# A new table of priority shifts for the list scheduler of a retention and SwiGLU kernel

## The chip, the cores and the metric

The kernel runs on one core of one Trainium2 chip. The metric is the device time of one execution in microseconds (us); three runs of the kernel before gave 630.61, 630.70 and 630.80, median 630.70. Engines are named as the profile names them: PE (matrix multiply), PEld (its weight loads), DVE (vector engine), ACT (scalar engine), POOL (GpSimd) and SP (the queue that issues most of the transfers).

## The reference

Two parts follow one another. Retention attention works on q, k, v of shape (4, 8, 768, 64) in blocks of 64 positions, with a decay `lam` for each of the 8 heads:

```python
for b in range(nb):                       # 12 blocks of 64
    intra = einsum('bhic,bhjc->bhij', qb, kb) * Dmask     # Dmask = lam ** (i-j), lower triangle
    intra = einsum('bhij,bhjd->bhid', intra, vb)
    inter = einsum('bhid,bhde->bhie', qb * lam_pow, kv_state)
    out[:, :, sl] = intra + inter
    kv_state = lam_block * kv_state + einsum('bhsd,bhse->bhde', kb * rev_pow, vb)
```

Its output, rearranged to 3072 tokens of 512 values, goes through a normalised SwiGLU layer with 1536 hidden values:

```python
xn = x / sqrt(mean(x * x, axis=-1) + 1e-6) * rms_g
g, val = xn @ w_gate, xn @ w_val
out = (g * sigmoid(g) * val) @ w_out
```

## The kernel before

The 3072 tokens are cut into six groups of 512 (`m` = 0 to 5) and the 1536 hidden values into twelve slices of 128 (`f` = 0 to 11). A unit is one slice of one group. Units run in the order: group 0 with slices 0 to 5, group 1 with all slices, group 0 with slices 6 to 11, then groups 2 to 5 with all slices; 72 in all.

A unit has products on PE, element work on ACT, DVE and POOL, and output products on PE. Values are split into a high and a low float16 part, so that a product is three passes.

- The first 24 units are classical: `gate` and `val` (L908) make pg and pv of 128x512, 12 matmuls each. ACT applies silu (L1172), DVE multiplies (L1179), ACT takes the high part hh (L1191), DVE the rest (L1202).
- The later 48 units use seven products of half size (L1098, `Product.add`), six matmuls of 128x256 each, which add up in two banks, pa and pb. Between two products that write one bank, ACT copies pa to `kept` (`keep`, L1146) or DVE adds pb to it (`sum_val`, L1150; `sum_gate`, L1154). Then ACT does silu (L1158), DVE multiplies (`mul_sums`, L1166), ACT takes the high part (`high`, L1191), DVE the low part (`low`, L1202).
- Output products (L927, L928, L929) add three matmuls of 128x512 for one slice and 128 tokens into one of four accumulators. When the last slice of a group is in, DVE or ACT takes the rows out (L953, L975) and a queue writes them. The last group also has block products (L1298).

The attention of the next group is laid between the units, a pair of heads at a time: scores (L543), state sums (L573), mix (L626), new states (L644), with DVE (L559, L592, L601, L607) and POOL (L563) work between. For group 0 it is done ahead of all units, in the first 25 us, by other functions: scores L683, state sums L714, mix L724, L734, and on DVE L698 and L601. The decay powers that it needs are scans on DVE (`powers`, L159 and L164); the largest value of `rms_g`, which sets the scales, goes DVE L196, PE L203, DVE L207 to L213. Weights are converted on ACT and DVE (L242, L251, L254, L487, L491), and POOL and DVE form the weight sums that the half-size products need (L1030, L1045 to L1049, L1067).

All this is written down as steps of a plan (`step(engine, cost, at, function, ...)`), each with what it reads, writes and newly opens. `at` is the step's due time in units. A list scheduler (`Plan.run`) keeps a clock for each engine and repeatedly starts, of the steps that are ready, one with a low `at`; no step is looked at whose `at` lies more than 1.3 ahead of the furthest PE step. The order that comes out is emitted as it is: each engine runs its instructions in that order, and semaphores make an instruction wait for what it needs. On each engine an instruction that waits holds up all behind it. Before the plan runs, a table changes the due times:

```python
for i, (eng, cost, at, *rest) in enumerate(plan.steps):
    plan.steps[i] = (eng, cost, round(at + SHIFTS.get(i, 0), 4), *rest)
order = plan.run()
```

Where the planner sees PE idle for long at the start, `busy` (L141) puts in matmuls that nobody reads.

Of the kernel before, what the change touches and what calls it, by code (L numbers as in the profile page):

```python
# [23 lines left out]
def retention_swiglu_kernel(  # L24
# [2037 lines left out]
    def load_steps():  # L2062
# [21 lines left out]
        66: 0.3, 67: 3.35, 68: 2.15, 77: 0.55, 82: 0.9, 83: 1.65, 84: 2.3, 88: 3.45, 101: -1.35,  # L2084
        104: 4.25, 113: 2.15, 121: 4.7, 128: 1.9, 129: -4.25, 130: 1.95, 135: 2.8, 138: 5.65, 139:
        5, 144: 5.5, 145: -10.4, 148: -10.2, 152: 1.55, 154: -0.1, 155: 0.8, 157: 6.9, 159: 1.35,
        160: -0.35, 161: 1.1, 163: 6.45, 171: 2, 172: 10.05, 175: 7.15, 185: 3.3, 187: 4.75, 192:
        1.35, 193: -7.95, 194: 5.35, 196: -2.4, 199: -2.9, 204: 0.75, 205: 2.75, 207: -0.6, 213:
        5.15, 232: 3.15, 236: 5.45, 241: 3.3, 245: -2.3, 251: -5.15, 252: 0.55, 255: 1.75, 260:
        -5.95, 263: 1.1, 264: 1.3, 265: -12.65, 269: -2.25, 271: 1.4, 274: -1.4, 276: 1.85, 277:  # L2090
        4.6, 279: 0.9, 281: -1.55, 282: 5.15, 287: -7.3, 289: 2.95, 290: 3.8, 291: -4.35, 292:
        -2.1, 298: -1.85, 300: -2.15, 302: -3.2, 303: 1.6, 306: -3.05, 308: -5.85, 313: -6.8, 315:
        0.9, 318: 3.05, 320: -0.7, 323: 3.8, 324: 5.05, 331: 1.65, 334: -0.75, 335: -1.2, 336:
        -7.75, 339: 0.5, 342: -2.25, 344: 1.55, 355: 6.1, 357: 2.25, 358: -2.55, 360: 1.65, 363:
        -2.05, 378: 6.35, 379: 7.1, 380: 7.8, 381: 8.9, 383: 0.1, 390: 9.1, 396: 9.6, 397: 5.95,
        398: 1.75, 411: -2.25, 416: 4.35, 418: 5.35, 422: 5.15, 426: 3.1, 434: 3.05, 435: 1.9,
        436: 4.55, 438: 3.85, 456: 2.95, 458: 4.55, 465: 5.1, 469: 5, 475: -0.2, 476: 2.4, 480:
        -1.5, 481: 1.1, 484: -12.15, 486: -12.35, 487: -5.15, 488: 1.25, 492: 1.65, 496: -2.95,
        502: -8.75, 509: 2.65, 510: -14.05, 514: 2.3, 515: 2.8, 516: 1.45, 518: -6.3, 519: -6.4,
        520: -2.75, 524: 1.45, 529: -3.45, 531: 1.75, 534: -7.25, 536: 2.3, 543: -9.05, 545: 1.2,  # L2100
        548: 1.6, 549: 0.7, 555: 6.65, 561: -3.85, 563: -2.7, 564: -1.9, 568: -3.8, 570: 1.6, 571:
        1.3, 572: 1.6, 573: 2, 574: -6.45, 575: -7.4, 576: 5.75, 580: -4.2, 582: 4.7, 592: 3.35,
        595: -3.1, 596: -1.85, 598: 0.65, 602: -9, 605: 5.85, 607: 1.6, 608: 1.65, 612: -5.85,
        613: -6.2, 615: -0.55, 616: 1.3, 617: 4.25, 620: -4.2, 621: 7.2, 622: 2.3, 626: 5.9, 637:
        -2, 641: -5.75, 642: -13.3, 655: -3.35, 656: -3.5, 665: -3.05, 669: 1.55, 671: -2.65, 672:
        -3.25, 673: 2.5, 675: -2.8, 684: -2.65, 686: 0.45, 688: -1.7, 691: 2.4, 693: 2.5, 694:
        2.9, 703: 2.7, 705: 2.7, 714: 1.55, 720: 1.3, 726: 5.75, 728: 6.25, 735: 1.8, 738: 4.1,
        744: 5.55, 747: 4.5, 751: 0.3, 752: -0.85, 755: 3.45, 756: 3.45, 764: 0.3, 765: 3.55, 767:
        0.45, 769: 1.3, 770: 1.5, 773: 5.55, 774: -2.4, 775: -5.15, 779: 1.95, 781: 0.65, 789:
        3.35, 793: -6.55, 796: -5.05, 797: -6.15, 799: 4.75, 800: 4.8, 804: -2.55, 807: 2.35, 809:  # L2110
        3.55, 813: -1.7, 815: -1.05, 816: 6.1, 817: 6.25, 818: 6.15, 820: 5.75, 822: 5.5, 823:
        1.4, 826: 2.4, 827: 5.05, 833: 4.85, 846: -0.2, 847: 3.85, 851: 5.8, 852: 5.1, 854: 4.8,
        856: -0.65, 857: 6.15, 862: -2.65, 867: 1.65, 870: 5.2, 876: 4.8, 886: -8.45, 887: -2.3,
        896: 4.85, 903: 2.7, 913: -2.8, 914: 5.3, 915: -2.35, 918: 5.45, 928: 1.6, 930: 3.95, 933:
        3.9, 936: 5.4, 937: 1.75, 939: 5.2, 946: 0.35, 948: 4.7, 950: -2.05, 953: 8.55, 955: 3.35,
        957: -0.85, 958: 4.35, 960: 5.3, 966: 0.3, 967: -0.75, 971: 2, 976: -2.9, 978: 3.25, 981:
        8.3, 984: -4, 993: -0.45, 996: 5.85, 999: 2.8, 1000: -0.45, 1009: -2.65, 1013: 2.15, 1018:
        -0.45, 1019: -4.4, 1021: -0.35, 1025: 5.25, 1026: -5.25, 1033: 6.3, 1040: 5.4, 1041: -1,
        1042: 0.7, 1047: 2.4, 1054: -5.4, 1055: 1.05, 1061: 0.6, 1069: 5.85, 1075: 5.05, 1078:
        4.4, 1081: 0.35, 1082: -1.05, 1086: -1, 1091: 0.95, 1096: 1.3, 1097: -1.05, 1098: 1.25,  # L2120
        1101: -1.3, 1110: 1.4, 1114: 4.6, 1116: 0.6, 1119: 7.8, 1122: -3.95, 1126: 1.3, 1131:
        4.95, 1139: -0.95, 1149: 6.95, 1155: -7.4, 1160: -2.45, 1161: 2.4, 1162: -1.55, 1164:
        -0.6, 1167: -0.4, 1171: -0.9, 1173: 6.9, 1178: 7.25, 1180: 6.75, 1184: 6.5, 1185: -3.15,
        1186: 6.35, 1187: 6.35, 1188: 4.35, 1192: -4.05, 1193: 8.8, 1194: 4.3, 1198: 6.5, 1201:
# [227 lines left out]
```

## Time and profile before

| | |
|---|---|
| Runs of the kernel before | 630.61, 630.70, 630.80 us |
| Profiled execution, first to last instruction (its span) | 629.9 us |
| What lies around the span, by the median of the runs | 0.8 us |
| PE busy | 619.8 us, 98% |
| DVE busy | 463.4 us, 74% |
| ACT busy | 368.3 us, 58% |
| POOL busy | 198.8 us, 32% |
| Clock granted to PE | 9 tenths or more in all 40 slices |

The profiled execution has no time of its own beside its span; the runs lie 0.7 to 0.9 us above it. Matmuls overlap, and their ends are modelled, so a busy PE is not a PE without pauses: the rows further down give starts, and two starts that lie further apart than the same two instructions do elsewhere show a pause even where the busy time shows none.

### The profile page before, as it was taken

Reading aid. Unit: us, or ns where it says so; the run is one execution under the profiler, and the core shown is the slowest. Engines: PE = TensorE matmul, PEld = TensorE weight load, DVE = VectorE, ACT = ScalarE, POOL = GpSimd, SP = SyncE. Lnnn points to the kernel's source line nnn. Section 1 sums busy time; section 2 is a strip of 40 time slices with the busy share of each in tenths; the row PEclk is TensorE's granted clock in tenths of the full one; section 3 lists DMA queues with packets and bytes.
Section 4 is the critical chain, followed back from the end, with each engine's and each line's share of the span. In section 5 each row is a group of like instructions: output and inputs, shape, how many; then the busy total and the mean of one; then the engine's idle time right before and its main releaser. Section 6 shows DMA issues by size and latency. Waiting matters only on the chain.

```text
span 629.9 us, 15419 instructions
## 1 busy us (share of the span) xinstructions
PE 619.8 (98%) x6376; PEld 422.5 (67%) x6376; DVE 463.4 (74%) x941; ACT 368.3 (58%) x775; POOL 198.8 (32%) x197
## 2 busy tenths in 40 slices
PE   8899999999999999999999999999999999999997
PEld 5646564555655545676777777776777677777885
DVE  6899998886579887966897445686555487676555
ACT  3899868766676564565645554535454435545442
POOL 2532130303386636676503111202113002551410
PEclk9999999999999999999999999999999999999999
DMA  8938555701010120121201422100320000100001
GB/s 329 375 119 287 197 202 201 234 3 68 15 55 2 50 84 1 69 69 68 69 0 52 136 85 69 69 0 2 119 86 2 1 2 2 51 1 18 2 1 68
DMA packets 14326, 51.33 MB, mean 81 GB/s; under 512 B 1712, under 2 KB 1968, under 8 KB 12848
## 3 DMA queue, kind: packets, MB, share of 16 engines
q1 hardware_dynamic: 13968, 50.21, 22.8%
q8 instruction: 50, 0.82, 0.5%
q10 hardware_dynamic: 288, 0.14, 0.1%
q14 instruction: 20, 0.16, 0.1%
HBM read 44.05 MB, written 6.29 MB: 80 GB/s over the span
## 4 chain that ended last, share of the span: by engine, by line
PE 90%; DVE 6%; ACT 2%; issue 0%; POOL 0%; DVEq 0%
PE pa L1098 19%; PE pb L1098 14%; PE pg L908 9%; PE pv L908 9%; PE acc L927 9%; PE acc L929 8%; PE acc L928 8%; PE blocks L1298 2%; PE po L626 2%; PE po L644 2%; PE pa L543 2%; PE po L573 1%; DVE sg L1166 1%; PE po L724 1%; DVE hh L1202 1%; PE pa L683 1%
## 5 line engine op out<-in xcount | busy, mean ns | idle before, releaser
L1146 ACT COPY tx<-pa 128x256 f32<-128x256 f32 x144 | 53.3, 370 | 85.2 <-PE pa L1098 74.6
L929 PE MATMUL acc<-wo,hh 128*128 128x512 f16 (+1 forms) x264 | 101.1, 383 | 0.0
L928 PE MATMUL acc<-wo,hh 128*128 128x512 f16 (+1 forms) x264 | 101.0, 383 | 0.0
L1150 DVE TENSOR_TENSOR tx<-pb,tx 128x256 f32<-128x256 f32 x96 | 40.7, 424 | 51.8 <-PE pb L1098 45.2
L927 PE MATMUL acc<-wo,hh 128*128 128x512 f16 x192 | 72.8, 379 | 0.4 <-DVE hh L1202 0.4
L908 PE MATMUL pv<-x,wv 128*128 128x512 f16 x288 | 70.2, 379 | 0.0
L908 PE MATMUL pg<-x,wg 128*128 128x512 f16 x288 | 69.0, 379 | 0.8 <-ACT x L870 0.7
L1098 PEld LDWEIGHTS <-wg 128*128 128x128 f16 x576 | 56.0, 98 | 16.9 <-issue 0.3
L1191 ACT CAST hh<-sg 128x512 f16<-128x512 f32 (+2 forms) x73 | 44.7, 612 | 34.1 <-DVE sg L1166 19.6
L1098 PEld LDWEIGHTS <-wo 128*128 128x128 f16 x576 | 55.8, 98 | 12.9 <-issue 0.6
L1098 PEld LDWEIGHTS <-wv 128*128 128x128 f16 x576 | 56.2, 98 | 11.3 <-DVE a L559 0.6
L563 POOL TENSOR_TENSOR qkv<-qkv,pw 128x512 f32<-128x512 f32 x20 | 27.1, 1355 | 109.7 <-PE pa L543 77.9
L1202 DVE TENSOR_TENSOR hh<-sg,hh 128x512 f16<-128x512 f32 x53 | 45.2, 854 | 8.9 <-ACT hh L1191 8.3
L908 PEld LDWEIGHTS <-wg 128*128 128x128 f16 x288 | 26.7, 98 | 33.5 <-issue 3.5
L908 PEld LDWEIGHTS <-wv 128*128 128x128 f16 x288 | 26.1, 98 | 32.2 <-issue 2.5
L1166 DVE SCALAR_TENSOR_TENSOR sg<-tx,cv,sg 128x512 f32<-128x512 f32 (+1 forms) x49 | 40.4, 824 | 9.6 <-ACT sg L1158 6.2
L1154 DVE TENSOR_TENSOR sg<-pb,tx 128x256 f32<-128x256 f32 x48 | 20.3, 423 | 32.7 <-ACT tx L1146 18.8
L1158 ACT ACTIVATE sg<-sg,cg 128x256 f32<-128x256 f32 x48 | 24.4, 508 | 31.9 <-DVE sg L1154 31.0
L902 POOL TENSOR_TENSOR tx<-xt,tx 128x768 f16<-128x768 f32 x8 | 14.8, 1854 | 80.4 <-ACT tx L898 70.1
L1098 PE MATMUL pb<-tx,wo 128*128 128x256 f16 x288 | 39.3, 272 | 0.2 <-DVE tx L1150 0.2
L1098 PE MATMUL pa<-x,wv 128*128 128x256 f16 x288 | 39.3, 273 | 0.1
L1098 PE MATMUL pb<-x,wg 128*128 128x256 f16 x288 | 39.3, 273 | 0.0
(241 smaller groups left out, 1301.5 us busy)
## 6 DMA issues: line engine op xcount, KB each, us to landing
qkv<-in_qkv_dram SPq DMA_DIRECT2D x48, 512.0 KB, 5.0
raw_gv<-in_weights_dram SPq DMA_DIRECT2D x11, 1024.0 KB, 6.5
raw_o<-in_weights_dram SPq DMA_DIRECT2D x12, 512.0 KB, 6.2
out_dram<-o SPq DMA_DIRECT2D x23, 256.0 KB, 2.1
partial<-in_weights_dram SPq DMA_DIRECT2D x2, 512.0 KB, 11.7
out_dram<-o ACTq DMA_DIRECT2D x1, 128.0 KB, 2.4
out_dram<-o SPq DMA_DIRECT2D x1, 128.0 KB, 2.8
cs<-in_consts_dram ACTq DMA_DIRECT2D x1, 8.0 KB, 4.3
```

Of the source, the lines that this page charges most:

```text
L563: eng.tensor_mul(self.qT, self.qT, by.broadcast_to([P, GC, P]))
L908: nc.tensor.matmul(ps, w[:, kk, :], x[:, kk, :], start=i == kk == 0, stop=i == 2 and kk == NK - 1,)
L927: nc.tensor.matmul(acc[:, cols], hl[:, ts_], oh, start=first, stop=False, skip_group_check=True)
L928: nc.tensor.matmul(acc[:, cols], hh[:, ts_], ol, start=False, stop=False, skip_group_check=True)
L929: nc.tensor.matmul(acc[:, cols], hh[:, ts_], oh, start=False, stop=last, skip_group_check=True)
L1098: nc.tensor.matmul(ps, w(ow, k), x(ox, k), start=first and i == k == 0, stop=i == 2 and k == 1, skip_group_check=True,)
L1146: nc.scalar.copy(self.kept[:, i], self.pa)
L1150: nc.vector.tensor_add(self.val[:, half], self.pb, self.kept[:, i])
L1158: nc.scalar.activation(self.sg[:, half], self.sg[:, half] if t else self.pa, AF.Silu, scale=cg[:, self.f, 0:1],)
L1166: nc.vector.scalar_tensor_tensor(sg, self.val[:, half], cv[:, self.f : self.f + 1], sg, ALU.mult, ALU.mult)
L1191: nc.scalar.copy(self.hh[:, half], self.sg[:, half])
L1202: nc.vector.tensor_sub(self.hl, self.sg, hh)
```

## The change

Only the table `SHIFTS` is another. It had 663 entries and has 562; 260 steps are in both, none with the same number. The mean size of a shift was 3.98 units and is 7.20. The steps, their costs, their functions and the scheduler are the same. Two lines of the table, of 86 that go and 72 that come:

```diff
     SHIFTS = {
-        66: 0.3, 67: 3.35, 68: 2.15, 77: 0.55, 82: 0.9, 83: 1.65, 84: 2.3, 88: 3.45, 101: -1.35,
...
+        56: 7.1, 60: 6.05, 61: 2.35, 62: 10.65, 65: 2.45, 66: 0.5, 73: 8.5, 75: 7.2, 77: 9.6, 78:
```

Every instruction of before is there once in the changed kernel: 8303 on PE, 943 on DVE, 755 on ACT, 202 on POOL and 99 on SP, branches included, with the same 7 unread matmul calls. What is new is the order on each engine, and with it which buffer of a pool a step gets and what it waits for. Three places follow. Names carry the group and the slice (`hh_2_0` is the hidden part of group 2, slice 0); the last number of a name only tells buffers apart, and lines after the table have numbers 14 lower in the changed kernel.

First, DVE at the start. `wv` holds the decay powers here, `a_0_0` the scores of the first pair of heads of group 0, `pst` its state sums. Before:

```order
L196 TENSOR_REDUCE gmax_128<-cs_94 128x1
L159 SCALAR_TENSOR_TENSOR wv_132<-cs_94,ident_111 128x128 x2
L164 SCALAR_TENSOR_TENSOR wv_132<-cs_94,wg_131 128x128
L159 SCALAR_TENSOR_TENSOR wv_132<-cs_94,ident_111 128x128 x2
L698 TENSOR_TENSOR a_0_0_168<-pa_0_0_0_149,wv_132 128x512
L698 TENSOR_TENSOR a_0_0_168<-pa_0_0_1_150,wv_132 128x512
L601 SCALAR_TENSOR_TENSOR a_0_0_168<-a_0_0_168,wv_132,pst_0_0_173 128x64 x3
L601 SCALAR_TENSOR_TENSOR state_122<-a_0_0_168,wv_132,pst_0_0_173 128x64
```

And in the changed kernel:

```order
L159 SCALAR_TENSOR_TENSOR wv_132<-cs_94,ident_111 128x128 x2
L164 SCALAR_TENSOR_TENSOR wv_132<-cs_94,wg_131 128x128
L159 SCALAR_TENSOR_TENSOR wv_132<-cs_94,ident_111 128x128 x3
L164 SCALAR_TENSOR_TENSOR wv_132<-cs_94,wg_131 128x128
L196 TENSOR_REDUCE gmax_128<-cs_94 128x1
L698 TENSOR_TENSOR a_0_0_183<-pa_0_0_0_149,wv_132 128x512
L698 TENSOR_TENSOR a_0_0_183<-pa_0_0_1_150,wv_132 128x512
L159 SCALAR_TENSOR_TENSOR wv_132<-cs_94,ident_111 128x128
L601 SCALAR_TENSOR_TENSOR a_0_0_183<-a_0_0_183,wv_132,pst_0_0_170 128x64 x3
L159 SCALAR_TENSOR_TENSOR wv_132<-cs_94,ident_111 128x128
L164 SCALAR_TENSOR_TENSOR wv_132<-cs_94,wg_131 128x128
L159 SCALAR_TENSOR_TENSOR wv_132<-cs_94,ident_111 128x128
```

The search for the largest value (L196) goes from the first place behind seven scans; two scans more stand ahead of the first pair's L698, one stands between its L698 and its L601, and the state sum of L601 goes further back. On PE, the two matmuls of L203 that wait for L196 move behind the first pair's state sums, and the scores of the second pair come in one run.

Second, DVE at about 261 us, where the half-size units of group 2 begin. Before:

```order
L559 TENSOR_TENSOR a_3_1_3270<-pa_3_1_1_3245,mask_124 128x256
L1150 TENSOR_TENSOR tx_1_2635<-pb_2_1_3117,tx_0_2634 128x256
L1166 SCALAR_TENSOR_TENSOR sg_2_1_3223<-tx_1_2635,cv_139,sg_2_1_3223 128x512
L1202 TENSOR_TENSOR hh_2_0_3198<-sg_2_0_3158,hh_2_0_3198 128x512
L1150 TENSOR_TENSOR tx_1_2635<-pb_2_2_3284,tx_0_2634 128x256
L592 TENSOR_TENSOR po_3_1_1_3294<-a_3_1_3270,po_3_1_1_3294 128x256
L601 SCALAR_TENSOR_TENSOR a_3_1_3270<-a_3_1_3270,both_123,po_3_1_1_3294 128x64 x3
L607 SCALAR_TENSOR_TENSOR a_3_1_3270<-a_3_1_3270,pw_125,po_3_1_0_3293 128x256
L601 SCALAR_TENSOR_TENSOR state_122<-a_3_1_3270,both_123,po_3_1_1_3294 128x64
L1202 TENSOR_TENSOR hh_2_1_3313<-sg_2_1_3223,hh_2_1_3313 128x512
```

And in the changed kernel:

```order
L975 SCALAR_TENSOR_TENSOR o_0_0_3276<-acc_0_6_0_2747,ik_140,partial_95 128x512
L1202 TENSOR_TENSOR hh_2_0_3231<-sg_2_0_3154,hh_2_0_3231 128x512
L1150 TENSOR_TENSOR tx_1_2639<-pb_2_1_3169,tx_0_2638 128x256
L1166 SCALAR_TENSOR_TENSOR sg_2_1_3257<-tx_1_2639,cv_139,sg_2_1_3257 128x512
L1150 TENSOR_TENSOR tx_1_2639<-pb_2_2_3286,tx_0_2638 128x256
L1202 TENSOR_TENSOR hh_2_1_3321<-sg_2_1_3257,hh_2_1_3321 128x512
L592 TENSOR_TENSOR po_3_1_1_3303<-a_3_1_3236,po_3_1_1_3303 128x256
```

The low part of slice 0 (L1202 `hh_2_0`) moves ahead of slice 1's L1150 and L1166, behind an accumulator's exit (L975); the low part of slice 1 moves ahead of the attention work of L592 to L607. On PE the output product that reads `hh_2_0` stood behind a product of slice 2 before:

```order
L1098 LDWEIGHTS wo16_2_2056
L1098 MATMUL pa_2_2_3275<-tx_1_2635,wo16_2_2056 128x256
L927 LDWEIGHTS hh_2_0_3198
L927 MATMUL acc_2_0_1_3341<-wo16_0_1959,hh_2_0_3198 128x512
L928 LDWEIGHTS hh_2_0_3198
L928 MATMUL acc_2_0_1_3341<-wo16_0_1959,hh_2_0_3198 128x512
L929 LDWEIGHTS hh_2_0_3198
L929 MATMUL acc_2_0_1_3341<-wo16_0_1959,hh_2_0_3198 128x512
L1098 LDWEIGHTS wo16_2_2056
```

and stands behind the second product of slice 2 and ahead of the attention run L626 in the changed kernel:

```order
L1098 LDWEIGHTS wv_132
L1098 MATMUL pb_2_2_3286<-x_2_1791,wv_132 128x256
L927 LDWEIGHTS hh_2_0_3231
L927 MATMUL acc_2_0_1_3297<-wo16_0_1997,hh_2_0_3231 128x512
L928 LDWEIGHTS hh_2_0_3231
L928 MATMUL acc_2_0_1_3297<-wo16_0_1997,hh_2_0_3231 128x512
L929 LDWEIGHTS hh_2_0_3231
L929 MATMUL acc_2_0_1_3297<-wo16_0_1997,hh_2_0_3231 128x512
L626 MATMUL po_3_1_0_3302<-a_3_1_3236,qkv_3_1_3078 64x64 x2
```

So both its producer and its reader are earlier. The next reader, of `hh_2_1`, stands behind the attention runs of this place (L626, L573) and one more output product.

Third, PE at about 545 us, slice 1 of the last group. Before, the product that writes `pb_5_1` follows the one that writes `pa_5_1` directly:

```order
L1098 MATMUL pa_5_1_6933<-tx_0_2634,wo16_1_2030 128x256
L1098 LDWEIGHTS wo16_1_2030
L1098 MATMUL pa_5_1_6933<-tx_0_2634,wo16_1_2030 128x256
L1098 LDWEIGHTS wo16_1_2030
L1098 MATMUL pb_5_1_6943<-tx_0_2634,wo16_1_2030 128x256
L1098 LDWEIGHTS wo16_1_2030
L1098 MATMUL pb_5_1_6943<-tx_0_2634,wo16_1_2030 128x256
```

And in the changed kernel:

```order
L1098 MATMUL pa_5_1_6925<-tx_0_2638,wo16_1_2026 128x256
L1098 LDWEIGHTS wo16_1_2026
L1098 MATMUL pa_5_1_6925<-tx_0_2638,wo16_1_2026 128x256
L927 LDWEIGHTS hh_4_11_6869
L927 MATMUL acc_4_0_1_5872<-wo16_11_2842,hh_4_11_6869 128x512
L928 LDWEIGHTS hh_4_11_6869
L928 MATMUL acc_4_0_1_5872<-wo16_11_2842,hh_4_11_6869 128x512
L929 LDWEIGHTS hh_4_11_6869
L929 MATMUL acc_4_0_1_5872<-wo16_11_2842,hh_4_11_6869 128x512
L1098 LDWEIGHTS wo16_1_2026
L1098 MATMUL pb_5_1_6934<-tx_0_2638,wo16_1_2026 128x256
L1098 LDWEIGHTS wo16_1_2026
L1098 MATMUL pb_5_1_6934<-tx_0_2638,wo16_1_2026 128x256
```

An output product of the group before stands between them. Of such places in the last group, where only one product of six matmuls lies between two products into `pb`, there were ten, and two are left.

## Rows read from the trace of the kernel before

**Rows 1.** the page: busy time of PE; the chain that ended last, by engine.
```profile
PE 619.8 (98%) x6376; PEld 422.5 (67%) x6376; DVE 463.4 (74%) x941; ACT 368.3 (58%) x775; POOL 198.8 (32%) x197
...
PE 90%; DVE 6%; ACT 2%; issue 0%; POOL 0%; DVEq 0%
```

**Rows 2.** stretches: us, busy of each engine, granted clock, DMA share, GB/s.
```profile
5.11:23.94 18.83, 17.93 (x255) 14.35 (x256) 17.62 (x46) 9.63 (x19) 9.56 (x13) 1.00 1.02 393
246.00:312.00 66.00, 65.20 (x799) 47.18 (x798) 49.36 (x97) 37.08 (x91) 42.80 (x42) 1.00 0.19 65
312.00:526.00 214.00, 214.00 (x2465) 157.43 (x2463) 140.55 (x271) 107.30 (x247) 33.88 (x35) 1.00 0.14 46
526.00:615.00 89.00, 88.94 (x722) 70.11 (x720) 59.00 (x124) 45.05 (x94) 29.47 (x23) 1.00 0.04 13
```

**Rows 3.** waits of PE after 34 us: in total, times, longest.
```profile
PE acc L927 <- DVE hh L1202: 0.4, 1, 0.4
PE pb L1098 <- DVE tx L1150: 0.2, 1, 0.2
```

**Rows 4.** timeline of PE, first and last pause: start us, us, instruction.
```profile
123.18 1.24 PE L908 MATMUL pv<-x,wv 128*128 128x512 f16 x5
124.51 0.16 PE L345 MATMUL pc<-ones_b,sq_w 128*128 128x1 bf16 x1
...
613.61 0.81 PE L1098 MATMUL pa<-tx,wo 128*128 128x256 f16 x6
614.32 0.81 PE L1098 MATMUL pb<-tx,wo 128*128 128x256 f16 x6
614.97 0.82 PE L1098 MATMUL pa<-tx,partial 128*128 128x256 f16 x6
```

**Rows 5.** timeline of all engines near 262 us.
```profile
261.58 1.83 DVE L1166 SCALAR_TENSOR_TENSOR sg<-tx,cv,sg 128x512 f32<-128x512 f32 x1
261.59 1.27 POOL L563 TENSOR_TENSOR qkv<-qkv,pw 128x512 f32<-128x512 f32 x1
...
263.33 1.16 DVE L1202 TENSOR_TENSOR hh<-sg,hh 128x512 f16<-128x512 f32 x1
...
263.35 0.83 PE L1098 MATMUL pa<-tx,wo 128*128 128x256 f16 x6
...
264.54 0.39 PE L927 MATMUL acc<-wo,hh 128*128 128x512 f16 x1 [0.37 <-DVE hh L1202]
```

**Rows 6.** timeline of all engines near 545 us.
```profile
544.56 0.75 DVE L1166 SCALAR_TENSOR_TENSOR sg<-tx,cv,sg 128x512 f32<-128x512 f32 x1
...
545.16 0.81 PE L1098 MATMUL pa<-tx,wo 128*128 128x256 f16 x6
545.34 0.62 ACT L1191 CAST hh<-sg 128x512 f16<-128x512 f32 x1 [0.23 <-DVE sg L1166]
545.44 0.42 DVE L1150 TENSOR_TENSOR tx<-pb,tx 128x256 f32<-128x256 f32 x1
545.92 0.82 PE L1098 MATMUL pb<-tx,wo 128*128 128x256 f16 x6
545.99 0.69 DVE L1202 TENSOR_TENSOR hh<-sg,hh 128x512 f16<-128x512 f32 x1
```

**Rows 7.** timeline of DVE, then of POOL, first 34 us.
```profile
5.18 0.73 DVE L159 TENSOR_TENSOR_SCAN wv<-cs,ident 128x128 f32<-128x128 f32 x2
...
6.14 1.79 DVE L159 TENSOR_TENSOR_SCAN wv<-cs,ident 128x128 f32<-128x128 f32 x2
...
6.38 1.27 POOL L701 TENSOR_TENSOR qkv<-qkv,wv 128x512 f32<-128x512 f32 x1 [4.69 <-PE pa L683]
...
22.12 2.09 POOL L174 COPY mask<-wv 64x256 f32<-64x256 f32 x2
```

**Rows 8.** chain that ended last, first 34 us: start us, us, what.
```profile
22.95 0.59 ACT x L741
```

**Rows 9.** timeline of the last microseconds.
```profile
625.29 0.48 DVE L964 SCALAR_TENSOR_TENSOR o<-acc_right,ik,others 128x256 f32<-128x256 f32 x1
```

156 rows, old and new, of the table SHIFTS are left out of this document.

## The prediction, made before the changed kernel ran

> **What bounds the kernel now.** I read the page first: PE is busy 98% of the span and holds 90% of the chain that ended last; DVE has 6%, ACT 2% [rows 1]. So the kernel is a stream of matmuls that hardly stops, and an order can win only what PE waits. Next the stretches: PE is idle 0.80 of 66 us between 246 and 312, nothing between 312 and 526, 0.06 of 89 between 526 and 615; the granted clock is 1.00 throughout, its upper level of 2.4 GHz, so nothing is to be had there [rows 2]. The table of waits names only 0.4 and 0.2 us for PE after 34 us [rows 3].
>
> Both views are too small, because a matmul's record runs on after the next one has started. So I went to the timeline and read starts. Six half-size matmuls take 0.65 us from the first start to that of the next product (614.32 to 614.97); between 613.61 and 614.32 the same six took 0.71, a pause of 0.06 that no busy time shows. Five matmuls of 512 columns stand as 1.24 from 123.18; the record of one is 0.39 long [rows 5], so their starts are (1.24 - 0.39) / 4 = 0.21 apart and the sixth was due at 124.25; it starts at 124.51, a pause of 0.25 or so [rows 4]. These are the last and the first of 16 such pauses after 34 us. They add to 2.9 us: 0.47 in two before 246, 1.67 in six between 246 and 312, 0.09 in one at 353, 0.71 in seven between 526 and 615. The largest, 0.54, lies at 264.54: six half-size matmuls from 263.35 are over at 264.00 [rows 5]. Two further pauses just before 34 us stand behind work on DVE and ACT whose order the change leaves as it is, so they stay.
>
> **The change part by part.** No instruction comes or goes, and the attention matmuls, which cost PE extra where they alternate with wide ones, come in 52 runs in both orders. So PE's own work is the same, and the terms are the start, the 2.9 us of pauses, new pauses, and the end.
>
> *Start.* Up to 24 us DVE is busy 17.62 of 18.83 us [rows 2]; the path ends when PE has given ACT the last pair at 22.95 [rows 8]. The new order puts seven scans instead of five ahead of the first L698, which makes the first pair later by two scans; at 0.37 each (0.73 for two) that is 0.7. It takes the second pair's two L698 out from behind L207 to L213, which makes that pair earlier by about the same. DVE's total is the same, so I expect the last pair at the old time. The bound below is -0.1. Above: a pair of scans took 0.73 us beside nothing on POOL and 1.79 beside POOL's L701 [rows 7]; POOL's two mask copies of L174 (2.09 together) move from the end of this part to its middle, beside the scan and the steps L207 to L213 on DVE. One more pair stretched so costs 1.79 - 0.73 = 1.06, so +1.0. I take +0.25, near the lower end, since the copies do nearly the same total on POOL and something else on DVE is then alone.
>
> *34 to 246 us.* The two pauses (0.47) stand behind DVE. In the new order more matmuls lie between the producer and the reader at both. Three new places are close (a pv product of group 1 slice 3 behind L1179, and two others), each within 0.1 of a pause. Range -0.47 to +0.5; I take -0.25.
>
> *246 to 312 us.* This is where the half-size units begin while weight sums run on POOL and DVE. In the trace, DVE's L1166 begins at 261.58 and takes 1.83 us, beside POOL's L563; only then comes L1202 at 263.33, 1.16 us, and the output product waits until 264.54 [rows 5]. Alone the same two take 0.75 and 0.69 [rows 6]. The new order has `hh_2_0`'s L1202 ahead of that L1166, and its reader about 1.5 us earlier on PE. So the wait moves rather than ends: behind the L975 in front of it, L1202 ends 0.3 ahead of its reader at 0.69 and 0.2 behind it at 1.16. I count 0.25 of the 0.54 as won. What is late next is `hh_2_1`: L1150, L1166, ACT's L1191, L1150, L1202. Undisturbed that is 0.42 + 0.75 + 0.62 + 0.69, with some 0.1 between each, 2.9 us; PE has about 3.2 us of other work meanwhile (two products of 0.65 each, two attention runs of some 0.6 each, one output product 0.65). It fits by 0.3, and with both DVE operations stretched (1.08 and 0.47 more) it misses by about 1.2. The other two places of this kind, the product `pb_2_1` with wo and the output of `hh_5_1`, would miss by 0.3 and 0.6 with the durations that the trace has there now. So the new pauses lie between 0 and 2.1, and the old 1.67 go in whole or to the half: -1.67 to +1.0 net. I take -0.45.
>
> The Trainium skill, page GPSIMD Engine Reference, section Key points, says that POOL shares its SBUF interfaces with DVE and contends with DVE instructions that have two SBUF inputs. The 1.83 and 0.75 us above agree with it [rows 5, 6]. It speaks against this part of the change, since any new place beside POOL is a new long one; the third rival below is that case.
>
> *312 to 526 us.* PE shows no idle time [rows 2], one pause of 0.09. By the trace's durations the order has 137 places with under 0.5 us to spare instead of 109, but 78 instead of 76 under 0.2. Range -0.09 to +0.6, taken 0.
>
> *526 to 615 us.* A product into `pb` must wait until L1150 has added the one before. PE starts six matmuls at 545.16; L1150 runs from 545.44 to 545.86; the next product into `pb` starts at 545.92 [rows 6], 0.76 after 545.16 where 0.65 would do: 0.11. Ten places of the last group had just six matmuls in between, now two do; elsewhere an output product of 0.65 more covers it. Range -0.71 to 0; I take half, -0.35, since some of the seven pauses have other causes.
>
> *End.* The last DVE step begins at 625.29 [rows 9]. The new order puts DVE's L939 directly ahead of it, where DVE has been idle. 0, at most +0.25.
>
> *SP's queue.* Loads keep their sequence; outputs change places among themselves, and none is waited for. 0.
>
> The sum: +0.25 - 0.25 - 0.45 + 0 - 0.35 + 0 = -0.8 us, from 629.9 to 629.1 us of span. The runs' median lies 0.8 above the span of the profiled execution; kept, that gives 629.9 us. All low ends together give -3.0 (627.7), all high ends +3.35 (634.1).
>
> **The rivals.**
>
> *More is won.* All pauses between 246 and 312 go, all of the last group and the 0.47 before: -2.85, with the start at +0.25 it is -2.6, 628.1 us. For it: at every one of the old places I find more PE work between producer and reader in the new order. Against it: between 246 and 312 that holds only with undisturbed DVE durations, and POOL is busy 42.8 of 66 us there [rows 2].
>
> *The change does nothing.* The pauses come back elsewhere in the same size: 630.7 us. For it: the chain is PE for 90% [rows 1], and new close places are as many as the old. Against it: the last group's places are plainly fewer.
>
> *Slower, by DVE beside POOL.* The three new chains at `pb_2_1`, `hh_2_1` and `hh_5_1` meet POOL's L563, L1030 or L1067 and pay 0.3 + 1.0 + 0.6 = 1.9, the other old pauses stay, the start pays 0.5 and the last group gives 0.35 back: +2.05, 632.75 us. It decides from the point where the chains pay more than the last group and the start give, that is from about two of the three in full. For it: L1166 took 1.83 there already [rows 5]. Against it: the attention scores of this place stand some 3 us earlier, and L563 with them, so that it may run out before L1166 begins.
>
> **How the numbers follow.** A measurement of this kernel can tell about 0.2%, 1.26 us, from no change: faster is below 629.4, slower above 632.0. Chances: the forecast 0.42, more won 0.26, nothing 0.14, slower by DVE beside POOL 0.18. Of the forecast's 0.42 about a third lies below 629.4, since its centre is only 0.5 above that line; of the slower case 0.02 stays within. Faster: 0.26 + 0.14 = 0.40. Slower: 0.16 and 0.02 for the new close places between 312 and 526, 0.18. Within: 0.42. The range at 8 in 10 is 627.7 to 632.2: the low end is all low ends together, the high end leaves out the upper half of the slower case. The forecast's own range is 628.9 to 630.9.
>
> **What would show it.** In the profile after: the first L908 starts within 0.3 us of where it does now; PE's idle time between 246 and 312 is below 0.8 and in the last stage nothing; no product into `pb` of the last group starts 0.76 after the one before it, except at two places; the wait of L927 on L1202 at about 262 us is below 0.3. Wrong if the first L908 moves by more than 1 us, if L1166 of `sg_2_1` still takes 1.8 and PE waits for `hh_2_1`, or if pauses above 0.2 appear between 312 and 526.

## The result, and the profile after

The changed kernel takes 634.79 us in the median of four runs (633.56 to 635.68); the ratio to the kernel before is 1.0059, 95% interval 1.0043 to 1.0074. It is slower by some 4 us; 629.9 was forecast, in a range of 627.7 to 632.2, with 0.18 for slower. The profiled execution took 635.37 us, its span is 633.6. So 1.8 us lie around a span, and in all eleven experiments it is 1.8 or 1.9 as well; the 0.8 of the section on the kernel before came from setting the span of one execution against the runs of others. The execution that was traced before took some 631.7 us by this, 1.0 more than the three runs. Beside the experiments the kernel before gave 630.6 to 632.5 us, mostly near 630.8 or near 631.8.

The page of the changed kernel, busy time and the chain by engine, to hold against [rows 1]:

```profile
PE 620.2 (98%) x6376; PEld 422.7 (67%) x6376; DVE 466.0 (74%) x941; ACT 367.3 (58%) x775; POOL 193.2 (30%) x197
...
PE 79%; DVE 10%; ACT 6%; DMA 3%; issue 2%; POOL 1%; DVEq 0%; ACTq 0%
```

PE is busy 0.4 us longer, and that is all the first line tells. The chain tells more: PE holds 79% of it instead of 90%, DVE 10% instead of 6%. PE now waits for element work. The stretches, in the columns of [rows 2]:

```profile
246.00:312.00 66.00, 63.99 (x811) 45.97 (x811) 49.44 (x94) 38.38 (x93) 40.82 (x40) 1.00 0.19 63
312.00:526.00 214.00, 213.17 (x2452) 156.28 (x2450) 140.06 (x269) 105.75 (x244) 34.81 (x36) 1.00 0.14 47
526.00:615.00 89.00, 88.45 (x718) 69.98 (x717) 60.46 (x125) 45.52 (x96) 31.40 (x24) 1.00 0.04 13
```

PE's idle time grew from 0.80 to 2.01 us in the first of these, from nothing to 0.83 in the second, and from 0.06 to 0.55 in the third. Read from start to start, as in the prediction, the pauses after 34 us add to 7.5 us in 17 places, against 2.9 in 16. The difference, 4.6, is all but 0.1 of how much later the last DVE step begins: 629.97, against 625.29 [rows 9]. The spans differ by 3.7 only, because the end behind that step became 1.0 shorter (see End, below). PE's waits after 34 us, the longer ones, against [rows 3]:

```profile
PE pb L1098 <- DVE sg L1154: 1.2, 2, 0.6
PE acc L927 <- DVE hl L1202: 0.8, 1, 0.8
...
PE pa L1098 <- ACT tx L1146: 0.6, 1, 0.6
PE pb L1098 <- DVE tx L1150: 0.5, 1, 0.5
```

Mostly the instruction that such a wait names is not slow itself. One of them, followed back in the timeline of all engines near 336 us of the changed kernel:

```profile
336.05 1.64 POOL L902 TENSOR_TENSOR tx<-xt,tx 128x768 f16<-128x768 f32 x1 [17.38 <-ACT tx L898]
336.09 2.15 DVE L881 SCALAR_TENSOR_TENSOR yt<-x,gs,hy 128x512 f32<-128x512 f32 x1
...
338.28 0.62 ACT L870 CAST x<-yt 128x512 f16<-128x512 f32 x1 [1.09 <-DVE yt L881]
...
338.80 0.36 ACT L1146 COPY tx<-pa 128x256 f32<-128x256 f32 x1
...
339.22 0.81 PE L1098 MATMUL pa<-tx,wo 128*128 128x256 f16 x6 [0.56 <-ACT tx L1146]
```

L881 takes 2.15 us here; the same six instructions take at most 0.75 in the kernel before. It starts 0.04 behind POOL's L902 and ends at 338.24, 0.55 behind L902's end at 337.69. ACT's L870 waits for L881, the keep (L1146) stands behind L870, and the product that writes `pa` behind the keep: a pause of 0.72. The same near 555 us, in the last group:

```profile
554.49 2.72 POOL L1253 TENSOR_TENSOR out_parts<-out_sums,out_parts 128x512 f16<-128x512 f32 x2 [1.74 <-ACT out_parts L1249]
...
554.84 1.36 DVE L1166 SCALAR_TENSOR_TENSOR sg<-tx,cv,sg 128x512 f32<-128x512 f32 x1
...
556.80 0.60 PE L1098 MATMUL pb<-tx,wo 128*128 128x256 f16 x4 [0.55 <-DVE tx L1150]
```

Seven of the 17 pauses begin so, with a DVE operation of two inputs in SBUF that POOL was just ahead of: at 125.55, 254.81, 282.08, 286.51, 339.22, 362.62 and 556.80, 4.4 us together. An eighth, 0.72 at 306.55, has such an operation ahead of it too, but what DVE's L1154 waits for there is a buffer that POOL's L670 has to free:

```profile
306.07 0.42 DVE L1154 TENSOR_TENSOR sg<-pb,tx 128x256 f32<-128x256 f32 x1 [0.21 <-POOL sq L670]
```

L670 stands behind a POOL L1030 that met an L1202 and took 1.60 us, where its median is 1.16. So it is the same meeting of POOL and DVE with POOL as the late one; the expectations below count all eight, 5.2 us. One, 0.94 at 90.33, begins with a load:

```profile
85.07 0.67 ACT L242 ACTIVATE wv<-raw_o 128x512 f32<-128x512 f32 x1 [1.05 <-DMA raw_o<-in_weights_dram]
...
85.77 0.43 DVE L251 TENSOR_SCALAR wv<-wv 128x512 int32<-128x512 int32 x1 [1.31 <-ACT wv L242]
```

ACT and with it DVE stand still for the weights of one slice, and what PE needs is queued behind that. Other runs of this order have this pause elsewhere (70.6 us) or not at all, which fits the 2 us between its fastest and slowest run. The other eight are of 0.26 or less, 1.5 together.

All this is not more stretching, but stretching in other places. One of the two operations concerned most often, before the change (minimum, median and maximum in ns):

```profile
L1166 DVE SCALAR_TENSOR_TENSOR sg<-tx,cv,sg x49: 478/751/1950, 254.6 to 619.6; 128x512 f32<-128x512 f32 x47, 128x256 f32<-128x256 f32 x2
```

and after:

```profile
L1166 DVE SCALAR_TENSOR_TENSOR sg<-tx,cv,sg x49: 474/752/1490, 258.2 to 622.6; 128x512 f32<-128x512 f32 x47, 128x256 f32<-128x256 f32 x2
```

The longest is even shorter after the change, and so it is for the other one, L1202. A table by line shows nothing of it.

### The profile page after: what moved, and what is told of

Same layout as the page of the kernel before. It is cut to its first block, busy times and chain, and to the rows that moved or that the text cites. A ratio compares the mean times of both kernels' runs of the same rounds, so it can differ in the third digit from the quotient of the medians.

```text
span 633.6 us, 15417 instructions
## 1 busy us (share of the span) xinstructions
PE 620.2 (98%) x6376; PEld 422.7 (67%) x6376; DVE 466.0 (74%) x941; ACT 367.3 (58%) x775; POOL 193.2 (30%) x197
## 4 chain that ended last, share of the span: by engine, by line
PE 79%; DVE 10%; ACT 6%; DMA 3%; issue 2%; POOL 1%; DVEq 0%; ACTq 0%
PE pa L1098 18%; PE pb L1098 13%; PE acc L927 8%; PE acc L929 7%; PE acc L928 7%; PE pv L908 7%; PE pg L908 7%; PE blocks L1298 2%; DMA qkv<-in_qkv_dram 2%; PE po L644 2%; PE pa L543 1%; PE po L626 1%; DMA raw_o<-in_weights_dram 1%; PE po L573 1%; DVE hh L1202 1%
## 5 line engine op out<-in xcount | busy, mean ns | idle before, releaser
L1146 ACT COPY tx<-pa 128x256 f32<-128x256 f32 x144 | 53.5, 371 | 94.4 <-PE pa L1098 83.1
L1150 DVE TENSOR_TENSOR tx<-pb,tx 128x256 f32<-128x256 f32 x96 | 40.7, 424 | 45.2 <-PE pb L1098 42.0
L908 PE MATMUL pg<-x,wg 128*128 128x512 f16 x288 | 69.7, 379 | 1.0 <-ACT x L870 0.7
L908 PE MATMUL pv<-x,wv 128*128 128x512 f16 x288 | 68.6, 379 | 0.0
L563 POOL TENSOR_TENSOR qkv<-qkv,pw 128x512 f32<-128x512 f32 x20 | 26.8, 1340 | 79.8 <-DMA qkv<-in_qkv_dram 24.5
L1202 DVE TENSOR_TENSOR hh<-sg,hh 128x512 f16<-128x512 f32 x53 | 44.0, 832 | 8.1 <-ACT hh L1191 7.3
L908 PEld LDWEIGHTS <-wg 128*128 128x128 f16 x288 | 26.5, 98 | 34.1 <-issue 4.0
L1166 DVE SCALAR_TENSOR_TENSOR sg<-tx,cv,sg 128x512 f32<-128x512 f32 (+1 forms) x49 | 41.1, 840 | 10.5 <-ACT sg L1158 6.8
L908 PEld LDWEIGHTS <-wv 128*128 128x128 f16 x288 | 26.4, 97 | 31.8 <-issue 1.4
L1154 DVE TENSOR_TENSOR sg<-pb,tx 128x256 f32<-128x256 f32 x48 | 20.3, 422 | 34.6 <-ACT tx L1146 22.9
L1098 PE MATMUL pa<-tx,wo 128*128 128x256 f16 x288 | 39.3, 272 | 0.6 <-ACT tx L1146 0.6
```

The lines of the kernel that those rows point to most:

```text
L563: eng.tensor_mul(self.qT, self.qT, by.broadcast_to([P, GC, P]))
L908: nc.tensor.matmul(ps, w[:, kk, :], x[:, kk, :], start=i == kk == 0, stop=i == 2 and kk == NK - 1,)
L1098: nc.tensor.matmul(ps, w(ow, k), x(ox, k), start=first and i == k == 0, stop=i == 2 and k == 1, skip_group_check=True,)
L1146: nc.scalar.copy(self.kept[:, i], self.pa)
L1150: nc.vector.tensor_add(self.val[:, half], self.pb, self.kept[:, i])
L1166: nc.vector.scalar_tensor_tensor(sg, self.val[:, half], cv[:, self.f : self.f + 1], sg, ALU.mult, ALU.mult)
```

## The experiments

The theory (A): POOL and DVE start their operations on the same data event; where POOL is first, DVE's operation with two SBUF inputs stands until POOL's ends; the new order puts such operations ahead of steps that PE waits for. The rivals: the new order itself is too close (its waits would be there without POOL), or its loads are late. Ratios are to the kernel before, run beside each experiment, and are what to go by.

**Halves of the two orders.** The order of the changed kernel up to about 250 us, then that of before, and the other way round:

```diff
-        order = plan.run()
+        rest = ordered(OTHER)
+        order = ordered(SHIFTS)[:1088]
+        done = {i for _, i in order}
+        order += [x for x in rest if x[1] not in done]
```

> The changed order up to the start of group 2 (about 247 us), the old order behind it. In the trace of the changed kernel the pauses of PE after 34 us add to 2.7 us ahead of that point (0.5 before) and to 5.0 behind it (2.5 before). Theory A (each pause is local, made where a DVE step that PE waits for stands behind a DVE step stretched by POOL): about 2.2 over the old kernel, 632.9. Theory B (the new DVE order as such is too tight, everywhere alike): in proportion to length, 40% of the loss, 632.3. Theory C (the loss comes from the weight load at 78 us that lands late and shifts all behind it): nearly the whole loss, 634.5, with the spread of the changed kernel.

> The old order up to the start of group 2, the changed order behind it. Theory A: about 2.4 us over the old kernel, 633.1, and a small spread between runs since no late load is in it. Theory B: 60% of the loss, 633.1. Theory C: no loss, 630.7.

New order first: 634.42 us, ratio 1.0050 (1.0037 to 1.0063). Old order first: 635.31, 1.0073 (1.0060 to 1.0086). Both more than expected, since the seam makes pauses that neither order has, 1.6 us in the one (0.96 at 253.75, and 0.86 instead of 0.25 at 260.48) and this one, 2.9, in the other:

```profile
249.87 0.81 PE L1098 MATMUL pa<-tx,wo 128*128 128x256 f16 x6 [2.71 <-ACT tx L1146]
```

So the totals prove little. The places do: away from the seam each half has the pauses that it has in its own kernel. Behind the old first half the pauses at 282, 286, 306, 339, 362 and 557 us stand with 0.42, 0.62, 0.72, 0.71, 0.44 and 0.71, and in front of the old second half those at 104, 108, 115 and 125 with 0.25, 0.28, 0.18 and 0.73. They are made on the spot, and not handed on from the start.

**POOL held back at four places of the changed kernel.** POOL copies four values of the DVE result first, so that its long operation starts behind DVE's and not beside it. The order on all engines stays:

```diff
+            if i in gates:
+                nc.gpsimd.tensor_copy(gate, gates[i]())
             fn(*args)
```

> The changed order, and at four places (282, 336, 360 and 554 us) a copy of four values on POOL ahead of a long POOL operation; the copy reads what DVE writes in the step that the plan lays ahead of it, so that POOL starts only then. No order of any other engine changes. Theory A: the four pauses behind those places (0.42, 0.72, 0.44, 0.71 us) go, 2.3 us together, less some 0.2 for later POOL results: 632.7. Theory B: the pauses stay, 634.8. Theory C: 634.8.

632.39 us, 1.0023 (1.0014 to 1.0032), as expected: by the medians 2.4 us of 4.1 come back with four copies, by the ratios 2.3 of 3.7. The place near 336 us again:

```profile
334.34 0.75 DVE L881 SCALAR_TENSOR_TENSOR yt<-x,gs,hy 128x512 f32<-128x512 f32 x1
...
335.14 0.19 POOL L2266 COPY gate<-yt 128x4 f32<-128x4 f32 x1 [18.23 <-DVE yt L881]
...
335.29 1.64 POOL L902 TENSOR_TENSOR tx<-xt,tx 128x768 f16<-128x768 f32 x1
...
336.75 0.82 PE L1098 MATMUL pa<-tx,wo 128*128 128x256 f16 x6
```

L881 takes 0.75 and the product starts without a wait; PE is busy 214.00 of 214 between 312 and 526. What is left lies elsewhere, some of it new: POOL's L1030 now meets an L1202 at 293.27 (1.69 us), and PE waits for it until 295.02.

**The load.** ACT's L242 and DVE's L251 of the late slice moved back behind other work, nothing else:

```diff
+        for step_, ahead_of in [(477, 241), (496, 497)]:
+            place = [i for _, i in order].index(step_)
+            x = order.pop(place)
+            order.insert([i for _, i in order].index(ahead_of), x)
```

> The changed order with two steps moved back: ACT's lift of the output weights of slice 7 (L242 at 85 us, which waits for a load) behind the two high parts that follow it, and DVE's L251 on the same tile behind four L865, L873, L1179 and L1202. Theory A with C for this one place: the pause of 0.94 at 90.3 us goes, 633.9, and the spread between runs falls from 2 us to a few tenths. Theory B: 634.8, since the same work stands on DVE. Theory C in full (all loss hangs on this load): 631.

A miss: 635.08 us, 1.0062 (1.0050 to 1.0074). The pause at 90.33 is gone, and another of 1.09 stands at 99.11, where a small matmul for the weight scales waits for ACT's L464, which comes late behind the conversions on DVE:

```profile
99.11 0.16 PE L469 MATMUL pn<-ssq,ones_b 128*128 128x2 bf16 x1 [0.93 <-ACT junk L464]
```

What was won was given back 9 us later, and the runs lie as far apart as before (634.08 to 635.71).

**The same cure for the kernel before.** Five of its POOL operations that start with or just ahead of a DVE operation, between 242 and 308 us, get the copy:

> The old order with POOL copies of four values ahead of five of its long operations, each reading what DVE writes in the step that the plan lays ahead of it: L1030 at 242.9 us behind L1202 of hh_0_10, L1067 at 254.6 behind L1166 of sg_2_0, L563 at 261.6 behind L1166 of sg_2_1, L1030 at 296.2 behind L1049, L1067 at 308.0 behind L1166 of sg_2_6. Theory A (POOL stretches DVE): the old kernel's own pauses of 0.22, 0.25, 0.53, 0.31 and 0.32 shrink, 1.0 to 1.6 us in all: 629.1 to 629.7 against 630.7. Theory B (order alone): no change, 630.7.

629.15 us, 0.9972 (0.9961 to 0.9982), as expected, and faster than both kernels. The stretch and the place of [rows 5]:

```profile
246.00:312.00 66.00, 65.89 (x810) 48.29 (x808) 47.70 (x99) 38.74 (x95) 43.57 (x48) 1.00 0.19 65
```

```profile
261.05 0.75 DVE L1166 SCALAR_TENSOR_TENSOR sg<-tx,cv,sg 128x512 f32<-128x512 f32 x1
...
261.93 0.52 POOL L2283 COPY gate<-sg 128x4 f32<-128x4 f32 x1 [0.82 <-DVE sg L1166]
...
262.41 1.27 POOL L563 TENSOR_TENSOR qkv<-qkv,pw 128x512 f32<-128x512 f32 x1
```

L1166 takes 0.75 instead of 1.83; POOL's L563 starts 1.36 us behind it instead of with it, and nobody misses it. The five pauses behind the five places are gone, 1.63 us; so these, too, were of this kind. What is left of the 1.67 us of this stretch is at 310.21, where 0.15 has become about 0.4, since PE's L816 now waits for a POOL result that comes later:

```profile
309.88 0.19 PEld L816 LDWEIGHTS pss<-sr,ones 128*128 128x128 f32 x1 [0.43 <-POOL sr L810]
```

**Two DVE steps and one of ACT moved, no copies.** In the changed kernel the stretched L1202 at 362 us goes behind the L559 that PE waits for; L881 at 336 us, with the ACT step that reads it, goes behind an L1154:

```diff
+        for step_, ahead_of in [(1556, 1604), (1422, 1499), (1429, 1499)]:
```

> The changed order without gates; on DVE L1202 of hh_3_0 is moved behind the second L559 at 362 us, and L881 at 336 us (with ACT's L870 that reads it) behind the L1154 that follows. POOL starts as before. Theory A: a stretched DVE step costs only where PE waits for a step behind it, so the two pauses (0.44 and 0.72) go although L1202 and L881 stay near 1.5 and 2 us: 1.2 us off, 633.6. Theory B: the same, 633.6. If the stretch as such costs time wherever it falls: 634.8.

633.42 us, 1.0038 (1.0025 to 1.0050), as expected: the pause at 362 is gone, that at 339 is 0.27. At 362 us L1202 is still stretched:

```profile
359.44 1.24 DVE L1202 TENSOR_TENSOR hh<-sg,hh 128x512 f16<-128x512 f32 x1
```

So there it is what stands behind a stretched operation that decides, not the stretching. The other place does not show this: moved back, L881 came so late that it took 0.74 again, and not the 2 us that were expected.

**Three more copies in the changed kernel.**

> The changed order with the four gates that took 2.4 us off and three more: L1030 at 118.8 us behind L274 of wo_9, L1030 at 252.8 behind L1046, L1030 at 293.3 behind L1202 of hh_2_4. Theory A: the pauses of 0.70, 0.79 and 0.91 behind them go, 2.0 to 2.4 us: 630.0 to 630.4. Theory B: 632.4 as with four gates.

A miss: 632.17 us, 1.0014 (1.0005 to 1.0023), hardly better than with four. Two of the three places are mended, but POOL's operations are as long as before and now fall upon the next ones on DVE (a new pause of 1.02 stands at 298.88); the third place:

```profile
122.95 1.62 POOL L1030 TENSOR_TENSOR r<-wg 128x512 f32<-128x512 f16 x1
...
123.48 1.64 DVE L254 SCALAR_TENSOR_TENSOR wv<-raw_o,wv 128x512 int32<-128x512 int32 x1
...
125.85 0.18 PE L469 MATMUL pn<-ssq,ones_b 128*128 128x2 bf16 x1 [1.10 <-DVE a L559]
```

L254 ends 0.55 behind L1030, L559 stands behind L254, and the pause of 0.74 at 125.55 has become one of 1.27.

**POOL work added beside L1166, a tenth of a microsecond late and early.** In twelve units between 379 and 510 us of the kernel before, where POOL is idle, it gets an addition that nobody needs. First with a small copy ahead of it:

```diff
+            if i in beside:
+                nc.gpsimd.tensor_copy(gate, fn.__self__.val[:, HG : HG + 4])
+                nc.gpsimd.tensor_add(extra, mask, mask)
```

> The old order with an extra POOL addition of 128x512 that nobody reads in twelve units of groups 3 and 4, released when L1150 of the unit has written its second half, so that it starts about where L1166 starts. Theory A: L1166 of these units takes 1.3 to 1.8 us instead of 0.75, and PE pauses where the next L1150 has under 0.6 us to spare: 1 to 5 us slower, 632 to 636. Theory B: no change, 630.7, since no order changes.

then without it, the addition itself reading what L1150 writes:

```diff
-                nc.gpsimd.tensor_copy(gate, fn.__self__.val[:, HG : HG + 4])
-                nc.gpsimd.tensor_add(extra, mask, mask)
+                nc.gpsimd.tensor_add(extra, fn.__self__.val, fn.__self__.val)
```

> The kernel before, with the 12 added POOL additions of the run before it (same units, same moment), but without the small copy ahead of them: each addition reads L1150's output itself, so that it starts some 0.15 us sooner, at or just before DVE's L1166, where it started 0.10 to 0.17 us behind it and left L1166 at 0.75 us while it took 1.54 itself. Theory E (only one of the two runs at a time, and the one that starts first keeps the other out to its end): at 7 or more of the 12 places L1166 takes 1.4 to 1.6 us (it ends 0.55 behind the addition, as at 254.56 and 261.58 of the kernel before) and the addition 1.0; the median of the 12 additions falls from 1.51 to about 1.05, and the time rises by 0.5 to 3 us over the kernel before. Theory S (the two share the access and slow one another in proportion to their overlap): the 0.15 us of more overlap change little, L1166 stays at 0.75 to 0.9 and the addition at 1.5, and the time stays within 0.5 us of that run, 632.0.

The first missed: 631.96 us, 1.0012 (1.0002 to 1.0021). The trace says why; the same unit, with the copy:

```profile
385.99 0.75 DVE L1166 SCALAR_TENSOR_TENSOR sg<-tx,cv,sg 128x512 f32<-128x512 f32 x1
```

```profile
386.10 1.54 POOL L2277 TENSOR_TENSOR extra<-mask 128x512 f32<-128x512 f32 x1
```

and without:

```profile
386.88 1.63 DVE L1166 SCALAR_TENSOR_TENSOR sg<-tx,cv,sg 128x512 f32<-128x512 f32 x1
```

```profile
386.92 1.04 POOL L2275 TENSOR_TENSOR extra<-tx 128x512 f32<-128x512 f32 x1 [5.45 <-DVE tx L1150]
```

With the copy POOL comes 0.11 behind, L1166 takes 0.75 and the addition 1.54; without it POOL comes 0.04 behind, L1166 takes 1.63 and the addition 1.04. With the copy eight additions start 0.10 to 0.17 behind L1166, and all eight L1166 stay at 0.75 or 0.76; without it seven start 0.04 behind, and all seven L1166 take 1.63. That the two additions read different tiles is not the reason: at 503.06 of the second run the addition comes 0.16 behind, and L1166 stays at 0.75; at 508.54 of the first it comes 0.06 ahead, and L1166 takes 1.52. The two do not share: one goes through and the other stands, and less than 0.1 us decides which. The time, 632.33 us, 1.0016 (1.0007 to 1.0026), is within what either theory allowed and parts nothing; the durations do. Seven times 0.88 us on DVE cost little, since most places of this stretch have work that covers it: PE's pauses between 312 and 526 us go from 0.6 to 1.1 (0.1 in the kernel before), and 0.44 of that, at 505.06, has another reason, an L1150 that must not write over what the addition still reads.

**POOL's reading left out, in both kernels.** POOL's large operations are replaced by two small copies, which keep what they wait for, and a write of zeros; the low parts and sums that they form are left out:

```diff
-            eng.tensor_sub(t[:, 1, i], self.xt, t[:, 0, i])
+            written("tensor_sub", eng, t[:, 1, i], self.xt, t[:, 0, i])
...
+        for t in (a, b):
+            t = corner(t)
+            eng.tensor_copy(gate16 if t.dtype == F16 else gate, t)
+        eng.memset(to if to.dtype == F16 else to.bitcast(F32), 0.0)
```

> The kernel before, in which POOL's large two-input operations (the low parts and sums that L302, L563, L670, L810, L873, L902, L1030, L1067, L1231 and L1253 form) are left out: in the place of each POOL copies four values of either input, which keeps what it waits for, and then only writes zeros. The order of everything is kept. Theory E (a POOL operation that reads SBUF keeps out a DVE operation with two SBUF inputs to its end): the stretched L1166 and L1202 are gone (their longest falls from 1.95 and 1.6 to at most 1.0 us), the pauses between 246 and 312 with them, and the time is 628.5 to 629.8 us, as with the copies put ahead of five POOL operations (629.15). Rival R (the stretching comes from how busy POOL and DVE are together, or costs nothing that matters): 630.5 to 631.5.

> The changed kernel with the same POOL operations left out in the same way. Theory E: of the pauses of the changed kernel after 34 us the eight that begin with a DVE operation stretched beside POOL (125.55, 254.81, 282.08, 286.51, 306.55, 339.22, 362.62, 556.80; 5.2 us together) go, those of late loads and the short ones stay, and the time is 629.0 to 631.0 us, within -1 to +1.5 us of the kernel before treated alike. Rival R (the new order itself, or its loads, costs the 4 us): it stays 3 to 5 us behind the kernel before treated alike, 632.5 to 634.5.

The old order takes 628.71 us, 0.9961 (0.9946 to 0.9976), the new one 628.10, 0.9951 (0.9934 to 0.9968): the 4 us between them are gone, and the new order is 0.6 ahead, within the spread of four runs each. The old order is as expected; the new one misses its range by 0.9 us on the fast side; the late load, which was to stay, is not in its trace. From start to start the pauses after 34 us are 1.1 us in the old order and 0.9 in the new one, where they were 2.9 and 7.5. L1166, which is line 1185 here, in the new order:

```profile
L1185 DVE SCALAR_TENSOR_TENSOR sg<-tx,cv,sg x49: 477/751/778, 254.8 to 615.4; 128x512 f32<-128x512 f32 x47, 128x256 f32<-128x256 f32 x2
```

and the stretches of the new order:

```profile
246.00:312.00 66.00, 66.00 (x814) 48.82 (x813) 42.57 (x95) 40.30 (x99) 31.01 (x117) 1.00 0.20 65
312.00:526.00 214.00, 214.00 (x2467) 157.37 (x2465) 135.51 (x272) 106.50 (x246) 23.65 (x77) 1.00 0.14 46
526.00:615.00 89.00, 89.00 (x727) 70.74 (x726) 54.51 (x121) 44.50 (x94) 20.92 (x70) 1.00 0.04 13
```

No L1166 is longer than 0.78, and PE has no idle time from 246 to 615 us. By itself this pair does not part reading from length, as the writes are shorter too (mostly 0.52 us, against 1.3). Single places do; from the trace of the old order, POOL's write and the L1166 that starts in it:

```profile
424.37 0.73 POOL L286 MEMSET tx<- 128x768 f16 x1
```

```profile
424.48 0.75 DVE L1185 SCALAR_TENSOR_TENSOR sg<-tx,cv,sg 128x512 f32<-128x512 f32 x1
```

Had it stood until the write's end, as behind a reading operation, and ended 0.55 later, it would have taken 1.17. In these two traces five L1166 start 0.11 to 0.22 us into such a write, and all take 0.75.

## Why the prediction was wrong

The step that failed is the count of close places: the new order was worked out with the durations that instructions had in the old one, and those that DVE's operations have beside POOL do not go with the instruction. The three terms of the middle, -0.25, -0.45 and 0, came out at +2.2, +1.2 and +1.2.

*The bound* was read rightly: a stream of matmuls, and an order can win or lose pauses, and what lies at the start and the end.

*Start, +0.25.* Right against the execution that was traced, but that one had a long start. The first L908 of the changed kernel, and of the kernel before:

```profile
30.98 0.90 PE L908 MATMUL pg<-x,wg 128*128 128x512 f16 x2 [0.34 <-ACT x L870]
```

```profile
30.92 0.90 PE L908 MATMUL pg<-x,wg 128*128 128x512 f16 x2 [0.26 <-ACT x L870]
```

They differ by 0.06. But the old start comes in two forms. In three of the six traces that have it, one of them this, a scan is stretched beside POOL's L701 [rows 7], and L908 starts at 30.9 to 31.2. In the other three POOL comes behind the scan, and L908 starts at 29.8 to 30.0; from the run with the added additions and their copies:

```profile
6.11 0.71 DVE L159 TENSOR_TENSOR_SCAN wv<-cs,ident 128x128 f32<-128x128 f32 x2
...
6.92 1.27 POOL L701 TENSOR_TENSOR qkv<-qkv,wv 128x512 f32<-128x512 f32 x1 [5.23 <-PE pa L683]
```

All seven traces with the new start have a stretched scan, and L908 at 30.8 to 31.0. The runs near 630.8 and 631.8 us lie as far apart as the two starts; and of the two kernels with additions, the execution traced with the short start took 631.46 (all of that kernel: 631.41 to 632.67), the one traced with the long start 632.88 (631.75 to 632.96). So the three runs of 630.7 probably had the short one (none of them was traced), and against them the new start costs about 1.0. The 1.06 that the prediction priced for a scan beside POOL was right, and it had already been paid in the trace that was read.

*34 to 246 us, -0.25.* Wrong by 2.5: the pauses here went from 0.5 to 2.7 us. 0.94 is the late load, which I did not look at, since loads kept their sequence; but the steps behind a load were moved. 0.74 at 125.55 begins with DVE's L331 and L334, each behind a POOL L1030 (one from 118.77, and the one shown):

```profile
118.93 1.29 DVE L331 TENSOR_TENSOR sq_w<-sq_w 128x512 bf16<-128x512 bf16 x1
...
120.27 1.61 POOL L1030 TENSOR_TENSOR r<-wg 128x512 f32<-128x512 f16 x1
...
120.78 1.25 DVE L334 TENSOR_TENSOR sq_w<-sq_w 128x256 bf16<-128x256 bf16 x1
```

Their means over the kernel before are 0.46 and 0.29 us.

*246 to 312 us, -0.45.* The mechanism was seen ("L1166 ... takes 1.83 us, beside POOL's L563"), and then three new chains were worked out with it, `pb_2_1`, `hh_2_1` and `hh_5_1`. The place of [rows 5] came out well; the same steps in the changed kernel:

```profile
263.59 0.68 DVE L1202 TENSOR_TENSOR hh<-sg,hh 128x512 f16<-128x512 f32 x1
...
264.68 0.38 PE L927 MATMUL acc<-wo,hh 128*128 128x512 f16 x1
264.76 0.75 DVE L1166 SCALAR_TENSOR_TENSOR sg<-tx,cv,sg 128x512 f32<-128x512 f32 x1
```

No wait, and L1166 takes 0.75. But at all other places the closeness was counted "with the durations that the trace has there now". Those are no property of an instruction: 1.83 or 0.75 is decided by whether POOL started just ahead, and the new order deals that anew, for POOL as for DVE. Six pauses of 2.9 us stand here now, four of them above 0.4, at none of the three places.

*312 to 526 us, 0.* The same step: 137 close places against 109 was counted with old durations and costed at nothing; two of them, L881 and an L1202 beside L902 and L563, cost 1.16. Pauses above 0.2 here were a sign of being wrong that the prediction had named.

*526 to 615 us, -0.35.* The seven small pauses did go, as worked out, and one of 0.71 came at 556.80 from POOL's L1253: net nothing.

*End and SP's queue, 0.* Wrong by 1.0, on the good side. From the end of the last DVE step to the end of the span it is 4.12 us before and 3.14 after; 4.12 to 4.14 in all six traces with the old end, 3.13 or 3.14 in all seven with the new one. The last output, in the page of before and of after (the last number is us to landing):

```profile
out_dram<-o SPq DMA_DIRECT2D x1, 128.0 KB, 2.8
```

```profile
out_dram<-o SPq DMA_DIRECT2D x1, 128.0 KB, 1.9
```

The outputs that change places do count: SP issues its last four within 1.80 us before and within 3.91 after, so that fewer are on their way together. That this is why the last one lands sooner was not tested.

So the traced executions differ by 0.1 at the start, 4.6 in pauses and -1.0 at the end, 3.7 in all. Against the runs of 630.7 the start is +1.0 and the sum 4.6; the median of the changed kernel lies 0.6 below its traced execution, which leaves the 4.1. By the 1.8 around a span the forecast of 629.1 for the span meant a run of 630.9, not of 629.9.

*The rivals.* The third one, slower by DVE beside POOL, was the mechanism. Its price of 2.05 was for three places (with 1.0 for `hh_2_1`, where the working had 1.2); it was eight, elsewhere. It got 0.18 because I asked whether three named places would be hit; the question was how many of all places where PE has little cover would be. Where POOL does not read, the new order is 0.6 ahead (628.10 against 628.71), which is no support for the forecast of -0.8: it is within the spread, and the pauses, on which the forecast rested, differ by 0.2 there.

The page of the Trainium skill that the prediction cited says that POOL contends with DVE operations of two SBUF inputs. Who wins is told in the Trainium skill on another page, SBUF — State Buffer, section Who interferes with whom: "Issue order, not op shape, decides who blocks", and only a POOL operation that reads SBUF does this. The traces agree: 1.63 and 1.04 us against 0.75 and 1.54 by 0.07 us of difference in start, and no L1166 above 0.78 where POOL mostly writes. Which one is first they tell only to 0.05 us: the seven L1166 that lost to an addition start 0.04 ahead of it by the profile.

## What to carry to other kernels

A duration in a trace that belongs to contention goes with the moment, not with the instruction: when an order changes, work with the undisturbed duration and the disturbed one at every place that has less cover than their difference. A scheduler that lays POOL's operation behind DVE's in its plan has not put it there, as long as both wait for the same data; a copy of four values does (0.19 us on POOL, in two of five places 0.5 to 0.6), and five of them made the old order 0.28% faster. Put them only where POOL has room behind, since a POOL operation that is pushed falls upon the next DVE operation.

## What the runs showed of the hardware

A 128x512 DVE operation on 32-bit values with two SBUF inputs that comes just behind a POOL operation ends 0.55 us after that: L1166 after L563 (1.83 us), L881 after L902 (2.15), L254 after L1030 (1.64), L1166 after the added addition (1.63). L1049 and L1046, of half the size, end 0.28 and 0.29 us after it. So what it costs is what POOL has left to do, plus a rest that goes with DVE's own size. The other way round the addition ended 0.90 us behind L1166 (1.54 instead of 1.04). Which of the two stands is decided within 0.02 us of the profile's start times. In the eleven traces in which POOL reads, 149 of DVE's L1166, L1202, L881 and L873 (128x512) start between 0.1 us behind and 0.3 us ahead of a two-input POOL operation of over 0.9 us: all 33 that start at most 0.052 ahead take 1.52 to 2.16 us, all 116 that start 0.069 ahead or more take 0.68 to 0.89. L1150, which has one input in PSUM, took 0.41 to 0.43 throughout.
